# Softmax batches without the exponential function: power of two times a squared quartic, spread over three engines

## The chip, the cores and the metric

One core of one Trainium2 chip runs the whole program. The metric is device time in microseconds (us) of one execution; lower is better. Engines are named as in the profile: PE (TensorE matmul), PEld (its weight load), DVE (VectorE), ACT (ScalarE), POOL (GpSimd), SP (the queue that issues the DMAs).

## The reference

```
x: 8 x 4096 x 192      weight_gen: 8 x 4096 x 8 heads x 7 taps
w   = softmax(weight_gen, axis=-1)               # exp(w - max) / (sum + 1e-9)
out[b, s, h] = sum_k w[b, s, h, k] * x_pad[b, s + k, h]     # a 7-tap filter over the sequence
h   = out.reshape(32768, 192) @ w_in             # w_in 192 x 2048
y   = (h * cos(h)) @ w_out                       # w_out 2048 x 192
```

## The kernel before, in words

Each of the 128 partitions holds 256 consecutive rows of the sequence. The work goes in 64 blocks of 4 rows a partition. A block passes these stages:

- **Softmax** (`softmax`, L187): taps of 16 rows, so of four blocks, are loaded at once (a tile of 128x896). DVE finds the maximum of each 7 taps (L200), POOL subtracts it (L202), ACT takes the exponential in place (L205), POOL sums the taps (`add_taps`, L181 and L184) and scales the sum (L213), DVE takes the reciprocal (L216), POOL multiplies (L222). Three small early batches fill the start; fifteen "steady" ones follow, with `early=False`.
- **Filter** (`attention`, L244): on POOL, for a block, seven products (L257) and six sums (L272), 13 instructions in all; the last sum completes the tile `xa`.
- **Transpose**: PE transposes `xa` row by row (L316) into spare columns of the accumulator `acc` of the output matmul; ACT copies `acc` to `part` (L439), ACT and POOL split the transposed rows into `x_hi` (L297) and `x_lo` (L299).
- **First matmul** for a pair of 128-column chunks of w_in (L337 and L354, into `h`), eight pairs a block, 512 pairs in all; then h*cos(h): ACT rounds (L364), DVE takes the fraction (L368), ACT the cosine by its sine function (L372), DVE multiplies (L375), ACT and DVE split the product into `ghi` (L382) and `glo` (L386).
- **Second matmul** (`ffn_out`, L416), six pairs later (`LAG = 6`), then `evacuate`: the copy to `part`, and on POOL the sums `part` (L456) and `fin` (L457).

The order of each engine's instructions is the order in which the Python code issues them; a manual dependency at the end fixes it. The main loop goes over pairs `i`. In each pass it issues ACT's and DVE's work on earlier pairs, then `products()` (PE), then one `next(sm)` when the pair's `step` is in `SOFTMAX`, then two steps of the filter, `next(bg)`. `step` counts the pairs from 0 to 31 within a cycle of four blocks; each steady softmax batch begins at step 0 and feeds the four blocks whose transposes start at step 22 of that cycle and 8, 16 and 24 pairs later. The filter of a block may be issued only when its taps are `ready` (set after L222) and when the block two before is transposed. `until_mixed` (L487) issues whatever is missing of a block's filter just before its first transpose.

ACT holds one function table at a time: the exponential and the sine are in different ones. At step 6 (`EXP`) the kernel issues a table load, the exponential and a load back (the two rows `ACT_TABLE_LOAD` at L205 and L372). Around it the order is changed by hand: at step 7 `products()` is issued earlier, at steps 8 to 10 PE's second matmul is cut in two, and at steps 7 to 9 the splits are held back.

Of the kernel before, what the change touches and what calls it, by code (L numbers as in the profile page):

```python
# [11 lines left out]
F32 = mybir.dt.float32  # L12
F32R = mybir.dt.float32r
I32 = mybir.dt.int32
# [23 lines left out]


F64_SCALE = 2.0 ** -112  # L40


@with_exitstack
def tile_softmax_conv_then_cos_ffn(
# [133 lines left out]
    def add_taps(t, out):  # L178
# [4 lines left out]
        for more in (three[:, :, 1], three[:, :, 2], t[:, :, 6]):  # L183
            nc.gpsimd.tensor_tensor(out=out, in0=old, in1=more, op=ALU.add)  # L184
            old = out

    def softmax(r0, r1, eng, early=True, to=None):  # L187
        n = (r1 - r0) * H
        if r0 == 0:
            t = const.tile([P, n, K], F32, name="taps0")  # L190
        else:
            tile_ = work.tile([P, RW * H, K], F32, name="taps")
            t = tile_[:, 0:n, :]
        nc.sync.dma_start(out=t.rearrange("p a k -> p (a k)"), in_=g_v[:, :, r0 * H * K:r1 * H * K])
        for b in range(r0 // R, r1 // R):
            taps[b] = t.rearrange("p (r h) k -> p r h k", h=H)[:, b * R - r0:(b + 1) * R - r0]
        yield
        top_ = work.tile([P, RW * H], F32, name="top")
        top = top_[:, 0:n]
        nc.vector.tensor_reduce(out=top, in_=t, axis=AX.X, op=ALU.max)  # L200
        yield
        eng.tensor_tensor(  # L202
            out=t, in0=t, in1=top.unsqueeze(2).broadcast_to([P, n, K]), op=ALU.subtract)
        yield
        nc.scalar.activation(out=t, in_=t, func=AF.Exp)  # L205
        yield
        den_ = work.tile([P, RW * H], F32, name="den")
        den = den_[:, 0:n]
        if early:
            nc.vector.tensor_reduce(out=den, in_=t, axis=AX.X, op=ALU.add)  # L210
        else:
            add_taps(t, den)
        (nc.vector if early else nc.gpsimd).tensor_scalar(  # L213
            out=den, in0=den, scalar1=1e-9, scalar2=TWO_PI, op0=ALU.add, op1=ALU.mult)
        yield
        nc.vector.reciprocal(out=den, in_=den)  # L216
        yield
        m = 0 if to is None else to.shape[1]
        if m:
            eng.tensor_tensor(  # L220
                out=to, in0=t[:, 0:m], in1=den[:, 0:m].unsqueeze(2).broadcast_to([P, m, K]), op=ALU.mult)
        eng.tensor_tensor(  # L222
            out=t[:, m:], in0=t[:, m:], in1=den[:, m:].unsqueeze(2).broadcast_to([P, n - m, K]),
            op=ALU.mult)
        ready.update(range(r0 // R, r1 // R))
# [18 lines left out]
    def attention(b, eng, ra=0, rb=R, home="pr", t=None, acc=None):  # L244
        xt = rows[b]
        if t is None:
            t = taps[b][:, ra:rb]
        n = rb - ra
        if b not in mixed:
            xa_ = work.tile([P, R, D], F32, name="xa")  # L250
            mixed[b] = xa_
        xa = mixed[b][:, ra:rb]
        if acc is None:
            acc = xa

        def product(k, dst):
            eng.tensor_tensor(  # L257
                out=dst.rearrange("p r (h g) -> p r h g", h=H),
                in0=xt[:, k + ra:k + rb, :].rearrange("p r (h g) -> p r h g", h=H),
                in1=t[:, :, :, k:k + 1].broadcast_to([P, n, H, G]), op=ALU.mult)  # L260

        product(0, acc)
        yield
        old = None
        for k in range(1, K + 1):
            if k < K:
                pr = work.tile([P, R, D], F32, name="pr", tag=home,
                               bufs={"pr": 2, "turn": TMP, "part0": 3}[home])
                product(k, pr[:, ra:rb])
                yield  # L270
            if old is not None:
                eng.tensor_tensor(out=acc if k < K else xa, in0=acc, in1=old[:, ra:rb], op=ALU.add)  # L272
                yield
            old = pr
# [53 lines left out]
    def ffn_in_first(i, h=None):  # L328

        b, pair = divmod(i, NPAIR)  # L330
        x_hi, x_lo = xT[b]
        if h is None:
            h = ps_h.tile([P, 2, CT], F32, name="h")
        for m, (w, v) in enumerate(((wa_hi, x_lo), (wa_lo, x_hi), (wa_hi, x_hi))):
            for q in range(2):
                rs = slice(q * D2, (q + 1) * D2)
                nc.tensor.matmul(  # L337
                    h[:, q, :], lhsT=w[rs, chunk(pair, q)], rhs=v[rs, q, :],
                    start=(m == 0), stop=False, skip_group_check=True)
        hs[i] = h  # L340
        traded(h)
# [86 lines left out]
    def evacuate(j):  # L428
        b, m = divmod(j, 2 * R)
        half, m = divmod(m, R)  # L430
        tp, s = divmod(m, 2)
        if s == 0:
            return
        group = j // 2
        acc = accs.pop(group)
        bt = group // R + 2
        part = work.tile([P, 2, CT], F32, name=f"part{half}", bufs=(3 if half == 0 else 2))
        if WHOLE < bt < NB:
            nc.scalar.copy(out=part, in_=acc)  # L439
            r = group % R  # L440
            splits.append(split(bt, part[:, :, 2 * D:], slice(r * P, (r + 1) * P), nc.gpsimd))
        else:
            nc.scalar.copy(out=part[:, :, 0:2 * D], in_=acc[:, :, 0:2 * D])
        part = part[:, :, 0:2 * D]
        if half == 0:
            sums[(b, tp)] = part
            return
        if tp == 0:
            fin_t = work.tile([P, R, D], F32, name="fin")
            finals[b] = fin_t  # L450
        fin = finals[b]
        old = sums.pop((b, tp))
        last = b == NB - 1
        eng = nc.vector if last else nc.gpsimd
        ts = slice(2 * tp, 2 * tp + 2)
        eng.tensor_tensor(out=part, in0=part, in1=old, op=ALU.add)  # L456
        eng.tensor_tensor(out=fin[:, ts, :], in0=part[:, :, 0:D], in1=part[:, :, D:2 * D],  # L457
                          op=ALU.add)
        if tp == 1 or last:
            t0 = 2 * tp if last else 0  # L460
            def store(t0=t0):
                nc.sync.dma_start(out=o_v[:, :, (b * R + t0) * D:(b * R + 2 * tp + 2) * D],
                                  in_=fin[:, t0:2 * tp + 2, :].rearrange("p r d -> p (r d)"))

            if last:
                store()
            else:
                stores[j + LATE] = store
        if tp == 1:
            finals.pop(b)  # L470
            for pair in range(NPAIR):
                g_parts.pop(b * NPAIR + pair)
# [94 lines left out]
    N = NB * NPAIR  # L567

    sm = sm2
    EXP = 6  # L570
    SOFTMAX = (0, 2, 3, EXP, 7, 12, 13)
    for i in range(N + LAG + 1):
        b, pair = divmod(i, NPAIR)
        j = i - LAG
# [3 lines left out]
        if step == 0 and b + 4 < NB:  # L578
            r0 = (b + 4) * R
            sm = softmax(r0, min(r0 + RW, RPP), nc.gpsimd, early=False)  # L580
        busy = b + 4 < NB if step < NPAIR else b + 3 < NB
        exps = busy and step == EXP
        converts_now = converts.get(i, ())
        if converts_now:
            make_room()
# [8 lines left out]
        def products():  # L594
            if b < NB and pair == 0:
                assert b in transposed
            if whole is not None and j >= 0:

                ffn_out(j)
                ffn_in_first(i, whole)  # L600
            elif busy and EXP + 2 <= step <= EXP + 4:

                ffn_out(j, rest=False)
                ffn_in_first(i)
                ffn_out(j, rest=True)
            else:
                if i < N:
                    ffn_in_first(i, whole)
                if j >= 0:
                    ffn_out(j)  # L610
            if i < N:
                ffn_in_second(i)
            if j in stores:
                stores.pop(j)()
            if j >= 0:
                evacuate(j)


        early_sums = busy and step == EXP + 1
        if 0 <= i - 1 < N:  # L620
            act_turns(i - 1)
        if early_sums:
            products()
        if 0 <= i - 2 < N:
            act_hi(i - 2)
        all_of(*converts.pop(i - 1, ()))
        if exps:
            next(sm)
        now, later = [], []
        if not (busy and EXP + 1 <= step <= EXP + 3):  # L630
            now = list(splits)
            splits.clear()
        if whole is not None:
            t = work.tile([P, 2, CT], F32, name="part0", bufs=3)
            nc.scalar.copy(out=t, in_=whole)
            later.append(split(b + 1, t, slice(0, CT), nc.vector))
        if 0 <= i - 1 < N:
# [12 lines left out]
        all_of(*now)  # L650
        if i == N + LAG:
            break
        if not early_sums:
            products()
        load_weights(i)
        if step in SOFTMAX and step != EXP or NPAIR - 2 <= i < NPAIR + 1:
            next(sm, None)
        for _ in range(3 if i < 12 or i < 64 and i % 4 == 0 else 2):
            next(bg, None)
# [41 lines left out]
```

## Time and profile before

| | |
|---|---|
| median of 3 runs | 2301.77 us (2301.21 to 2303.03) |
| span of the profiled execution | 2300.3 us, 1.5 us under that median |
| PE busy | 2215.2 us, 96% of the span |
| POOL busy | 2002.3 us, 87% |
| DVE busy | 1905.0 us, 83% |
| ACT busy | 1897.5 us, 82% |
| ACT table loads at L205 and L372 | 15 and 15, 1283 ns each |

The page gives busy time by engine and granted clock by slice. The timeline lists an engine's instructions with their start in us from the span's start, their length, and in brackets the idle time ahead of one and what ended it. Idle time of an engine that others do not wait for costs nothing.

### The profile page before, as it was taken

How to read it: one execution, taken by the hardware profiler on the slowest of the kernel's cores; microseconds unless marked ns; L12 is line 12 of the kernel's file. 1: busy time of each engine (PE TensorE's matmuls, PEld its weight loads, DVE VectorE, ACT ScalarE, POOL GpSimd, SP SyncE). 2: the span in 40 equal slices, each digit the busy share in tenths (PEclk: the TensorE clock that was granted, in tenths of full speed). 3: DMA queues.
4: the chain of work that ended last, by engine and by line, in shares of the span. 5: the costliest groups of instructions: out<-in, count | busy, mean ns of one | idle time of the engine just before them, and what ended most of it. 6: DMA issues, size and time to landing. Idle time of an engine off the chain costs nothing.

```text
span 2300.3 us, 60609 instructions
## 1 busy us (share of the span) xinstructions
PE 2215.2 (96%) x26504; PEld 1993.6 (87%) x26504; DVE 1905.0 (83%) x1646; ACT 1897.5 (82%) x2131; POOL 2002.3 (87%) x1461
## 2 busy tenths in 40 slices
PE   3799999999999999999999999999999999999998
PEld 2588998889888888998989988898888889899897
DVE  7788888888888888888888888888888888888886
ACT  4588888888888888888888888888888888888885
POOL 8699989999999989989899899989989899899840
PEclk8799999999999999999999999999999999999999
DMA  6211221211211211211211212212211212212100
GB/s 154 56 43 40 50 51 33 58 41 34 58 39 44 50 40 44 50 49 34 58 33 43 58 31 52 50 32 52 50 41 42 58 26 50 57 26 52 33 9 22
DMA packets 25767, 105.55 MB, mean 46 GB/s; under 512 B 2734, under 2 KB 6566, under 8 KB 25502
## 3 DMA queue, kind: packets, MB, share of 16 engines
q1 hardware_dynamic: 25502, 101.67, 18.5%
q8 instruction: 208, 3.41, 0.6%
q14 instruction: 57, 0.47, 0.1%
HBM read 76.50 MB, written 25.17 MB: 44 GB/s over the span
## 4 chain that ended last, share of the span: by engine, by line
PE 56%; POOL 22%; ACT 11%; DVE 7%; issue 4%; DMA 0%; SPq 0%; POOLq 0%; ACTq 0%; DVEq 0%
PE acc L416 26%; PE h L354 19%; PE h L337 10%; POOL pr L257 6%; POOL xa L272 6%; DVE turn L368 3%; ACT part L439 3%; ACT turn L364 3%; POOL part L456 3%; DVE glo L386 2%; POOL x_lo L299 2%; POOL xa L257 2%; POOL fin L457 2%; ACT turn L372 2%; ACT ghi L382 1%
## 5 line engine op out<-in xcount | busy, mean ns | idle before, releaser
L368 DVE TENSOR_TENSOR turn<-h,turn 128x1024 f32<-128x1024 f32 x512 | 625.8, 1222 | 309.9 <-ACT turn L364 309.9
L416 PE MATMUL acc<-wo,ghi 64*128 64x384 f32 x8144 | 815.2, 336 | 16.6 <-ACT part L439 13.5
L416 PEld LDWEIGHTS acc<-wo,ghi 64*128 64x128 f32 x8144 | 739.2, 185 | 64.2 <-ACT part L439 26.7
L272 POOL TENSOR_TENSOR xa<-xa,pr 128x768 f32<-128x768 f32 (+1 forms) x384 | 704.0, 1833 | 0.7
L372 ACT ACTIVATE turn<-turn 128x1024 f32<-128x1024 f32 x512 | 543.7, 1062 | 181.0 <-DVE turn L368 177.7
L375 DVE SCALAR_TENSOR_TENSOR h<-h,turn 128x1024 f32<-128x1024 f32 x512 | 631.0, 1232 | 54.2 <-ACT turn L372 54.2
L364 ACT ACTIVATE turn<-h 128x1024 int32<-128x1024 f32 x512 | 525.6, 1027 | 165.0 <-PE h L354 164.2
L386 DVE TENSOR_TENSOR glo<-h,ghi 128x1024 bf16<-128x1024 f32 x512 | 622.4, 1216 | 9.9 <-ACT ghi L382 9.9
L257 POOL TENSOR_TENSOR pr<-xt,taps 128x768 f32<-128x768 f32 (+1 forms) x384 | 588.2, 1532 | 11.9
L382 ACT CAST ghi<-h 128x1024 fp32r<-128x1024 f32 x512 | 518.2, 1012 | 15.5 <-DVE h L375 15.5
L416 PE MATMUL acc<-wo_b,glo 64*128 64x192 bf16 x8144 | 435.6, 243 | 0.0
L456 POOL TENSOR_TENSOR part<-part,part 128x768 f32<-128x768 f32 x126 | 233.0, 1849 | 183.0 <-ACT part L439 156.7
L416 PEld LDWEIGHTS <-glo 64*128 64x128 bf16 x8144 | 333.8, 94 | 28.5 <-issue 13.7
L337 PE MATMUL h<-x_lo,wa_hi 64*128 64x512 f32 x1024 | 216.4, 410 | 37.0 <-DVE glo L386 28.4
L354 PE MATMUL h<-x_lo,wa_hi 64*128 64x512 f32 x1024 | 251.1, 478 | 0.6
L439 ACT COPY part<-acc 128x1024 f32<-128x1024 f32 x244 | 242.9, 996 | 0.0
L354 PE MATMUL h<-x_lo,wb_hi 64*128 64x512 f32 x1024 | 209.4, 397 | 0.0
L354 PE MATMUL h<-x_hi,wa_hi 64*128 64x512 f32 x1024 | 209.1, 396 | 0.0
L337 PE MATMUL h<-x_hi,wa_hi 64*128 64x512 f32 x1024 | 208.1, 394 | 0.0
L337 PE MATMUL h<-x_hi,wa_lo 64*128 64x512 f32 x1024 | 207.4, 392 | 0.0
L354 PE MATMUL h<-x_hi,wb_hi 64*128 64x512 f32 x1024 | 206.9, 391 | 0.0
L354 PE MATMUL h<-x_hi,wb_lo 64*128 64x512 f32 x1024 | 206.4, 391 | 0.0
(69 smaller groups left out, 2097.7 us busy)
## 6 DMA issues: line engine op xcount, KB each, us to landing
xt<-in_x_dram SPq DMA_DIRECT2D x62, 960.0 KB, 6.9
out_dram<-fin SPq DMA_DIRECT2D x63, 384.0 KB, 3.4
taps<-in_weight_gen_dram SPq DMA_DIRECT2D x15, 448.0 KB, 4.7
raw<-in_moe_w_out_dram SPq DMA_DIRECT2D x8, 384.0 KB, 4.2
raw<-in_moe_w_in_dram SPq DMA_DIRECT2D x10, 256.0 KB, 10.0
xt<-in_x_dram SPq DMA_DIRECT2D x1, 768.0 KB, 10.3
xt<-in_x_dram SPq DMA_DIRECT2D x1, 540.0 KB, 5.7
raw<-in_moe_w_in_dram SPq DMA_DIRECT2D x4, 128.0 KB, 5.6
```

Source lines behind the costliest of these rows:

```text
L257: eng.tensor_tensor(out=dst.rearrange("p r (h g) -> p r h g", h=H), in0=xt[:, k + ra:k + rb, :].rearrange("p r (h g) -> p r h g", h=H), in ...
L272: eng.tensor_tensor(out=acc if k < K else xa, in0=acc, in1=old[:, ra:rb], op=ALU.add)
L337: nc.tensor.matmul(h[:, q, :], lhsT=w[rs, chunk(pair, q)], rhs=v[rs, q, :], start=(m == 0), stop=False, skip_group_check=True)
L354: nc.tensor.matmul(h[:, 1 - q, :], lhsT=w[rs, cs], rhs=v[rs, q ^ middle, :], start=False, stop=(m == len(prods) - 1), skip_group_check=True)
L364: nc.scalar.activation(out=t.bitcast(I32), in_=hs[i], func=AF.Identity, bias=0.25, scale=1.0)
L368: nc.vector.tensor_tensor(out=t, in0=hs[i], in1=t.bitcast(I32), op=ALU.subtract)
L372: nc.scalar.activation(out=t, in_=t, func=AF.Sin, bias=SIN_BIAS, scale=SIN_SCALE)
L375: nc.vector.scalar_tensor_tensor(out=hs[i], in0=hs[i], scalar=TWO_PI, in1=turns.pop(i), op0=ALU.mult, op1=ALU.mult)
L382: nc.scalar.copy(out=hi, in_=hs[i])
L386: nc.vector.tensor_tensor(out=lo, in0=hs.pop(i), in1=hi.bitcast(F32), op=ALU.subtract)
L416: nc.tensor.matmul(to, lhsT=g[rs, n, t * P:(t + 1) * P], rhs=w[rs, fc, :], start=(lo == 0 and c == 0 and (whole or s == 0)), stop=(lo == 1 ...
L439: nc.scalar.copy(out=part, in_=acc)
```

## The change

For the fifteen steady batches the exponential of t (t is at most 0) is computed as follows: n = t / ln 2 rounded to an integer, r = t - n ln 2, a quartic in r/2 as the product of two squared terms with constants added, squared once more, times 2^n, whose bits ACT makes by a scale and a bias. A constant factor that stays in the taps cancels in the division. Early batches keep the exponential. The steps are spread over one pair each.

```
+    def powers(t):
+        nc.scalar.activation(out=whole, in_=t, func=AF.Identity, scale=1.0 / LN_2)
+        yield
+        nc.vector.scalar_tensor_tensor(
+            out=t, in0=whole, scalar=-LN_2, in1=t, op0=ALU.mult, op1=ALU.add)
+        yield
+        nc.scalar.activation(out=side, in_=t, func=AF.Square, bias=a1, scale=0.5)
+        yield
+        nc.scalar.activation(out=t, in_=t, func=AF.Square, bias=a2, scale=0.5)
+        yield
+        nc.vector.tensor_scalar(out=side, in0=side, scalar1=b1, scalar2=None, op0=ALU.add)
+        yield
+        nc.scalar.activation(out=whole, in_=whole, func=AF.Relu, bias=ONE_BITS, scale=2.0 ** 23)
+        yield
+        nc.vector.scalar_tensor_tensor(
+            out=t, in0=t, scalar=b2, in1=side, op0=ALU.add, op1=ALU.mult)
+        yield
+        nc.scalar.activation(out=t, in_=t, func=AF.Square)
+        yield
+        nc.gpsimd.tensor_tensor(out=t, in0=t, in1=whole.bitcast(F32), op=ALU.mult)
+        yield
...
-        yield
-        nc.scalar.activation(out=t, in_=t, func=AF.Exp)
-        yield
+        if early:
+            yield
+            nc.scalar.activation(out=t, in_=t, func=AF.Exp)
+            yield
+        else:
+            eng.tensor_scalar(
+                out=t, in0=t, scalar1=0.0, scalar2=EXP_LEAST, op0=ALU.min, op1=ALU.max)
+            yield
+            yield from powers(t)
...
-    EXP = 6
-    SOFTMAX = (0, 2, 3, EXP, 7, 12, 13)
+    SOFTMAX = (0, 1, 2, 4, 5, 6, 8, 9, 10, 11, 12, 13, 14, 16, 18)
```

The tiles `whole` and `side` are new with one buffer each; `top` goes from two buffers to one and `part0` from three to two. The special order around step 6 (`EXP`, `exps`, `early_sums`, the held-back splits, the cut second matmul) is removed, so every pair is issued alike.

With the new list the batch's last step, L222 before, is issued at step 18 where it was at step 13.

ACT around the exponential, before: rows of steps 6 and 7. In the names, `turn` and `ghi` are the work of the cosine.

```order
L364 ACTIVATE turn<-h 128x1024
L382 CAST ghi<-h 128x1024
L205 ACT_TABLE_LOAD
L205 ACTIVATE taps<-taps 128x896
L372 ACT_TABLE_LOAD
L372 ACTIVATE turn<-turn 128x1024
L297 CAST x_hi<-part_17943 128x2x128
```

ACT at the same place of the program with the change, from the end of step 4; `whole` is the first of the five new ACT instructions, `side` the second.

```order
L338 CAST x_hi<-part_17885 128x2x128
L200 ACTIVATE whole<-taps 128x896
L405 ACTIVATE turn<-h 128x1024
L423 CAST ghi<-h 128x1024
L413 ACTIVATE turn<-turn 128x1024
L480 COPY part_18024<-acc 128x1024
```

The pair of table loads with the exponential between is gone, and one ACT instruction stands behind the `x_hi` of each of the steps 4, 6, 8, 10 and 12.

POOL at steps 13 to 18, before: the `fin` of step 13, then the batch's last multiplication (L222), then the filter of the batch's first block.

```order
L457 TENSOR_TENSOR fin<-part_14016 128x384
L222 TENSOR_TENSOR taps<-taps,den 128x896
L257 TENSOR_TENSOR xa<-xt,taps 128x768
L257 TENSOR_TENSOR pr<-xt,taps 128x768
L299 TENSOR_TENSOR x_lo<-part_14016,x_hi 128x2x128
```

POOL from the same `fin` on with the change.

```order
L498 TENSOR_TENSOR fin<-part_14073 128x384
L218 TENSOR_TENSOR taps<-taps,whole 128x896
L340 TENSOR_TENSOR x_lo<-part_14073,x_hi 128x2x128
L188 TENSOR_TENSOR three<-taps 128x384
L191 TENSOR_TENSOR den<-three 128x128
L191 TENSOR_TENSOR den<-den,three 128x128
L191 TENSOR_TENSOR den<-den,taps 128x128
L253 TENSOR_SCALAR den<-den 128x128
L340 TENSOR_TENSOR x_lo<-part_14215,x_hi 128x2x128
L340 TENSOR_TENSOR x_lo<-part_14351,x_hi 128x2x128
L263 TENSOR_TENSOR taps<-taps,den 128x896
L298 TENSOR_TENSOR xa<-xt,taps 128x768
```

The last multiplication (now L263) and the first product behind it moved behind the `x_lo` rows of steps 14, 16 and 18, which stood behind them before.

POOL at the end of that block's filter, before; the `x_lo` row is that of step 20, the first `part` and `fin` are those of step 19, the second those of step 21.

```order
L272 TENSOR_TENSOR xa_14021<-xa_14021,pr_14303 128x768
L456 TENSOR_TENSOR part1_14439<-part1_14439,part0_14158 128x2x384
L457 TENSOR_TENSOR fin_14441<-part1_14439 128x384
L272 TENSOR_TENSOR xa_14021<-xa_14021,pr_14373 128x768
L299 TENSOR_TENSOR x_lo_14173<-part1_14439,x_hi_14172 128x2x128
L456 TENSOR_TENSOR part1_14575<-part1_14575,part0_14301 128x2x384
L457 TENSOR_TENSOR fin_14441<-part1_14575 128x384
L257 TENSOR_TENSOR xa_14579<-xt_14163,taps_13104 128x768
```

And with the change, from the second `part` on.

```order
L497 TENSOR_TENSOR part1_14631<-part1_14631,part0_14351 128x2x384
L498 TENSOR_TENSOR fin_14490<-part1_14631 128x384
L298 TENSOR_TENSOR pr_14635<-xt_13656,taps_13159 128x768
L313 TENSOR_TENSOR xa_14421<-xa_14421,pr_14563 128x768
L298 TENSOR_TENSOR pr_14638<-xt_13656,taps_13159 128x768
L313 TENSOR_TENSOR xa_14421<-xa_14421,pr_14635 128x768
L298 TENSOR_TENSOR pr_14641<-xt_13656,taps_13159 128x768
L313 TENSOR_TENSOR xa_14421<-xa_14421,pr_14638 128x768
L313 TENSOR_TENSOR xa_14421<-xa_14421,pr_14641 128x768
L340 TENSOR_TENSOR x_lo_14225<-part1_14631,x_hi_14224 128x2x128
L298 TENSOR_TENSOR xa_14712<-xt_14566,taps_13159 128x768
```

Before, the block's last sum stood ahead of the `part` of step 21; now it is the seventh row behind that step's `fin`, ahead of the next block's first product.

More of the change, by code (lines that the diff above doesn't have):

```diff
@@ L40 @@
 F64_SCALE = 2.0 ** -112
+EXP_A = ((0.2721300161859934, 6.259058152201904), (1.7341319627121385, 0.787141348722592))
+EXP_UNIT = 0.04161451162765518 ** 2
+EXP_LEAST = -100.0
+LN_2 = math.log(2.0)
+ONE_BITS = float(127 * 2 ** 23)
 @with_exitstack
@@ L185, in add_taps @@
             old = out
+    def powers(t):
+        (a1, b1), (a2, b2) = EXP_A
+        whole_ = work.tile([P, RW * H, K], I32, name="whole", bufs=1)
+        side_ = work.tile([P, RW * H, K], F32, name="side", bufs=1)
+        whole, side = whole_[:, 0:t.shape[1]], side_[:, 0:t.shape[1]]
+        nc.scalar.activation(out=whole, in_=t, func=AF.Identity, scale=1.0 / LN_2)
[18 more added lines that the diff above has]
+        yield
     def softmax(r0, r1, eng, early=True, to=None):
@@ L197, in softmax @@
         yield
-        top_ = work.tile([P, RW * H], F32, name="top")
+        top_ = work.tile([P, RW * H], F32, name="top", bufs=1)
         top = top_[:, 0:n]
@@ L213, in softmax @@
         (nc.vector if early else nc.gpsimd).tensor_scalar(
-            out=den, in0=den, scalar1=1e-9, scalar2=TWO_PI, op0=ALU.add, op1=ALU.mult)
+            out=den, in0=den, scalar1=1e-9 / (1.0 if early else EXP_UNIT), scalar2=TWO_PI,
+            op0=ALU.add, op1=ALU.mult)
         yield
@@ L267, in attention @@
                 pr = work.tile([P, R, D], F32, name="pr", tag=home,
-                               bufs={"pr": 2, "turn": TMP, "part0": 3}[home])
+                               bufs={"pr": 2, "turn": TMP, "part0": 2}[home])
                 product(k, pr[:, ra:rb])
@@ L436, in evacuate @@
         bt = group // R + 2
-        part = work.tile([P, 2, CT], F32, name=f"part{half}", bufs=(3 if half == 0 else 2))
+        part = work.tile([P, 2, CT], F32, name=f"part{half}", bufs=2)
         if WHOLE < bt < NB:
@@ L580, in tile_softmax_conv_then_cos_ffn @@
             sm = softmax(r0, min(r0 + RW, RPP), nc.gpsimd, early=False)
-        busy = b + 4 < NB if step < NPAIR else b + 3 < NB
-        exps = busy and step == EXP
         converts_now = converts.get(i, ())
@@ L600, in products @@
                 ffn_in_first(i, whole)
[L601 to L605, printed above, removed]
             else:
@@ L616, in products @@
                 evacuate(j)
-        early_sums = busy and step == EXP + 1
         if 0 <= i - 1 < N:
             act_turns(i - 1)
-        if early_sums:
-            products()
         if 0 <= i - 2 < N:
@@ L626, in tile_softmax_conv_then_cos_ffn @@
         all_of(*converts.pop(i - 1, ()))
[L627 to L632, printed above, removed]
+        later = []
+        now = list(splits)
+        splits.clear()
         if whole is not None:
-            t = work.tile([P, 2, CT], F32, name="part0", bufs=3)
+            t = work.tile([P, 2, CT], F32, name="part0", bufs=2)
             nc.scalar.copy(out=t, in_=whole)
@@ L652, in tile_softmax_conv_then_cos_ffn @@
             break
-        if not early_sums:
-            products()
+        products()
         load_weights(i)
-        if step in SOFTMAX and step != EXP or NPAIR - 2 <= i < NPAIR + 1:
+        if step in SOFTMAX or NPAIR - 2 <= i < NPAIR + 1:
             next(sm, None)
```

## Prediction

> **What bounds the kernel now.** I read the page first.
>
> ```profile
> span 2300.3 us, 60609 instructions
> PE 2215.2 (96%) x26504; PEld 1993.6 (87%) x26504; DVE 1905.0 (83%) x1646; ACT 1897.5 (82%) x2131; POOL 2002.3 (87%) x1461
> PEclk8799999999999999999999999999999999999999
> ```
>
> PE is busy 96% of the span at full granted clock, so a gain can only come out of PE's small remainder; POOL, at 87%, is the next to be late. Next, PE's timeline in a quiet stretch (seven pairs lie between these two pair starts), then around one exponential, step 7 to step 11 of the cycle, with two copies of ACT waited for and, later, an `x_lo` of POOL.
>
> ```profile
> 1238.04 0.43 PE L337 MATMUL h<-x_lo,wa_hi 64*128 64x512 f32 x2
> 1267.77 0.42 PE L337 MATMUL h<-x_lo,wa_hi 64*128 64x512 f32 x2
> ...
> 1167.62 0.40 PE L337 MATMUL h<-x_lo,wa_hi 64*128 64x512 f32 x2
> 1168.31 1.57 PE L416 MATMUL acc<-wo,ghi 64*128 64x384 f32 x16
> 1172.32 1.67 PE L416 MATMUL acc<-wo,ghi 64*128 64x384 f32 x16 [0.29 <-ACT part L439]
> 1182.23 1.67 PE L416 MATMUL acc<-wo,ghi 64*128 64x384 f32 x16 [0.63 <-ACT part L439]
> 1186.60 0.42 PE L337 MATMUL h<-x_lo,wa_hi 64*128 64x512 f32 x2
> 1208.26 0.49 PE L337 MATMUL h<-x_lo,wa_hi 64*128 64x512 f32 x2 [0.25 <-POOL x_lo L299]
> ```
>
> A quiet pair takes (1267.77 - 1238.04) / 7 = 4.247 us. Around the exponential four pairs take 1186.60 - 1167.62 = 18.98 us, 2.0 over 4 x 4.247. The whole cycle is seen in the rows of the table loads, one for each of the fifteen steady batches:
>
> ```profile
> L205 ACT ACT_TABLE_LOAD  x15: 1283/1283/1283, 196.7 to 2134.4; - x15
> ```
>
> (2134.4 - 196.7) / 14 = 138.4 us a cycle against 32 x 4.247 = 135.9: the exponential and all that goes with it cost PE **2.5 us a batch, 15 x 2.5 = 37 us** in all. That is the most that removing it can bring. Last, POOL's and PE's timelines from the batch's last multiplication (L222) to the first transpose of the block that it feeds, at step 22.
>
> ```profile
> 1202.62 1.77 POOL L222 TENSOR_TENSOR taps<-taps,den 128x896 f32<-128x896 f32 x1
> 1204.46 1.54 POOL L257 TENSOR_TENSOR xa<-xt,taps 128x768 f32<-128x768 f32 x1
> ...
> 1226.35 1.83 POOL L456 TENSOR_TENSOR part<-part,part 128x768 f32<-128x768 f32 x1
> 1228.26 1.03 POOL L457 TENSOR_TENSOR fin<-part 128x384 f32<-128x384 f32 x1
> 1229.25 1.85 POOL L272 TENSOR_TENSOR xa<-xa,pr 128x768 f32<-128x768 f32 x1
> 1231.06 0.74 POOL L299 TENSOR_TENSOR x_lo<-part,x_hi 128x256 fp32r<-128x256 f32 x1
> ...
> 1233.81 0.41 PE L337 MATMUL h<-x_lo,wa_hi 64*128 64x512 f32 x2
> 1235.92 0.23 PE L316 MATMUL acc<-ident,xa 64*128 64x64 f32 x2
> ...
> 1237.04 1.55 POOL L257 TENSOR_TENSOR xa<-xt,taps 128x768 f32<-128x768 f32 x1
> ```
>
> POOL needs 1229.25 + 1.85 - 1202.62 = 28.5 us from the start of L222 to the block's last sum, and ends it at 1231.10. PE, whose step 22 begins at 1233.81, reads the sum at 1235.92. So this chain has **4.8 us of slack**, about one pair. This is the view that decides my forecast.
>
> **The change part by part.**
>
> *The table loads and the exponential go.* ACT's rows at steps 6 and 7:
>
> ```profile
> 1164.49 1.01 ACT L382 CAST ghi<-h 128x1024 fp32r<-128x1024 f32 x1
> 1165.52 1.28 ACT L205 ACT_TABLE_LOAD   x1
> 1166.82 0.96 ACT L205 ACTIVATE taps<-taps 128x896 f32<-128x896 f32 x1
> 1167.79 1.28 ACT L372 ACT_TABLE_LOAD   x1
> 1169.09 1.06 ACT L372 ACTIVATE turn<-turn 128x1024 f32<-128x1024 f32 x1
> ```
>
> They hold up the cosine by 1169.09 - 1165.52 = 3.6 us; 2.5 of it and of the late `x_lo` reaches PE. Nothing else fills that place, so the 2.5 us come back. The Trainium skill, "ScalarE: Activation LUTs", section "What ACT_TABLE_LOAD costs", adds a drain of about 1.38 us to each load, 2.66 us a switch. Here each row begins 0.02 us behind the load ahead of it, so no drain shows; by the page the delay would be 6.3 us a batch, and by these rows it is 3.6.
>
> *Five ACT instructions and three on DVE come in,* at steps 4 to 12. The nearest ACT row is the exponential, 0.96 us for the same tile, some 0.1 of it overlapped as with its neighbours. For DVE the nearest is the maximum over a tile of that size, and above it the operations on `h`:
>
> ```profile
> L200 DVE TENSOR_REDUCE top<-taps 128x128 f32<-128x896 f32 x15 | 16.1, 1076 | 0.0
> L368 DVE TENSOR_TENSOR turn<-h,turn 128x1024 f32<-128x1024 f32 x512 | 625.8, 1222 | 309.9 <-ACT turn L364 309.9
> ...
> 1220.33 0.39 ACT L297 CAST x_hi<-part 128x256 fp32r<-128x256 f32 x1
> 1221.29 1.03 ACT L364 ACTIVATE turn<-h 128x1024 int32<-128x1024 f32 x1 [0.57 <-PE h L354]
> 1224.58 1.00 ACT L439 COPY part<-acc 128x1024 f32<-128x1024 f32 x1
> ```
>
> ACT has 0.57 us of idle time behind the `x_hi` of an even step and none in an odd one, so each new 0.87 us leaves it 0.3 us later: 1.5 us after five. DVE idles 310 / 512 = 0.6 us a pair, so 1.1 us put into a pair holds the cosine up by about 0.5 us there. PE forgives little: the copy ends at 1225.58, and the next second matmul starts 1168.31 - 1167.62 = 0.69 us into its pair; that pair starts at 1233.81 - 2 x 4.247 = 1225.32, so 0.43 us of lateness are free. Delay of 1.5 us, half a us more where DVE's instructions fall, less 0.4: I put 1.2 us a batch on PE, between 0 (all absorbed) and 2.5 (no better than the exponential). With the 2.5 us that come back, **the gain of this half is 1.3 us a batch**, from 0 to 2.5.
>
> *On POOL the batch's end moves by five steps.* The clamp, new at step 2, costs POOL between nothing and the 1.77 us of L222 on the same tile; it delays the sum of the block before, and a chain with 4.8 us of slack takes that. From step 13 on the product with `whole`, the sums over the taps and the scaling stand in a stretch where POOL now has no filter to work on, since no block has `ready` taps; the wait for what follows covers them. The last multiplication stands behind the `x_lo` of step 18, and that waits for ACT's `x_hi` of that step: step 18 begins at 1233.81 - 4 x 4.247 = 1216.82, and its `x_hi` is the row above, ended at 1220.72. With 0.74 us for the `x_lo` POOL starts the multiplication at 1221.5 instead of 1202.62, **18.9 us later**, on the clock of these rows. The way from there to the last sum has the same 14 instructions, but the order shows one `x_lo` in it instead of four (3 x 0.7 us less) and two `part` and `fin` instead of one (2.9 us more, from the start of that `part` to the next row): 28.5 + 0.8 = 29.3 us. The last sum so ends at 1221.5 + 29.3 = 1250.8. PE reads it at 1235.92 and can do nothing else, since its queue is in order: behind the transpose stand the rest of that pair and all later ones, and ACT and DVE then starve. **PE waits 14.8 us a batch.** The bounds are 13.3 and 16.3: 5% of the 29.3 us, since POOL runs beside other work there than in these rows.
>
> *PE's clock after such a wait.* At the program's start PE resumes after a wait of 3.64 us; the same work, first matmul to the second half of the first, stands there again a pair later:
>
> ```profile
> 95.00:101.50 6.50, 5.17 (x38) 4.73 (x40) 4.00 (x6) 1.89 (x4) 6.24 (x5) 0.50 0.00 0
> 101.50:108.00 6.50, 6.50 (x75) 5.72 (x72) 3.32 (x3) 4.70 (x7) 3.32 (x3) 0.99 0.43 96
> ...
> 96.33 0.80 PE L337 MATMUL h<-x_lo,wa_hi 64*128 64x512 f32 x2 [3.64 <-DVE glo L386]
> 101.52 0.53 PE L354 MATMUL h<-x_lo,wa_hi 64*128 64x512 f32 x2
> 103.03 0.41 PE L337 MATMUL h<-x_lo,wa_hi 64*128 64x512 f32 x2
> 105.76 0.49 PE L354 MATMUL h<-x_lo,wa_hi 64*128 64x512 f32 x2
> ```
>
> The granted clock is 0.50 in the first stretch and 0.99 in the second; the work takes 101.52 - 96.33 = 5.2 us against 2.7. A wait four times as long should do the same: **2.4 us a batch**, from 0 (it does not drop) to 3.2 (all 6.5 us of the first stretch at half speed). The Trainium skill, "TensorE: Matmul & The Clock Gate", section "What's actually happening", lifts the half clock after about 3.4 us of busy time, which would cost 1.7 us a batch and 10 us less in all; the row here has 5.2 us of it.
>
> *The rest has one answer.* `part0` loses a buffer: its two tiles are read by POOL before the wait is over, so ACT's copies find them free. The special order of steps 7 to 10 goes with the exponential and is in the 2.5 us. The next block's filter starts an `x_lo`, 0.7 us, behind the end of the wait; now it starts 1237.04 - 1235.92 = 1.1 us behind that transpose. On SP the load of the block's rows moves behind a store, whose `fin` POOL has done by then, and it lands in 6.9 us, issued while POOL is in the middle of the 29 us chain. Two more rows carry this and the next sum:
>
> ```profile
> L222 POOL TENSOR_TENSOR taps<-taps,den 128x224 f32<-128x224 f32 x1 | 0.6, 577 | 0.0
> ...
> xt<-in_x_dram SPq DMA_DIRECT2D x62, 960.0 KB, 6.9
> ```
>
> The sum: 15 x (14.8 + 2.4 - 1.3) = 238.5 us, less 1.2 us because the last batch's L222 is on a quarter of the tile (0.58 us, not 1.77), so 237 us on the span of 2300.3. The median is 1.5 us above the span: **2539 us**.
>
> **The rivals.**
>
> *POOL's chain does not bind (faster, 5%).* If PE's first transpose did not need this filter at step 22, only the other half would be left: 15 x 1.3 = 19.5 us less, 2282 us (2265 with all 2.5). It decides at L222's start: later than 4.8 us is too late, and the order says 18.9. Against it: the chain above, where every link is a row. The page's 2.66 us a switch, all on PE's path, would be 80 us for thirty switches and a time near 2220; the 37 us that the cycle shows over quiet pairs exclude it.
>
> *The wait without the clock (7%).* The same 14.8 us, but the granted clock stays at 1.0: 15 x 2.4 = 36 us less, 2503 us. For it: only the start, where PE works in short pieces, shows the drop.
>
> *The lateness is handed on (6%).* The filter of the next block is issued later too, with one more product, sum and `x_lo` (1.5 + 1.9 + 0.7 = 4.1 us) behind the `part` of step 27, which waits for ACT. If its slack is now 4.8 us, 0.7 are left. Should it miss by 3 us, 15 x 3 = 45 us come on top: 2584 us.
>
> *The new instructions eat the gain and no more (2%).* With ACT and DVE costing PE 2.5 us and no wait on POOL: 2302 us.
>
> **How the numbers follow.** My forecast has the remaining 80%. With all low ends it would be 15 x (13.3 + 0 - 2.5) = 162 us more, with all high ends 15 x (16.3 + 3.2) = 292; that they all meet is unlikely, so I take 2495 to 2585, which takes in the second and third rival. A measurement of this kernel tells about 0.2%, 5 us, from no change. Faster: the first rival and no other, 0.05. Same: 0.01. Slower: 0.94.
>
> **What would show it.** PE's idle time ahead of the transposes (L316 before) named to POOL's `xa` sum, about fifteen times 15 us; a granted clock that drops fifteen times; only the first two table loads left; and cycles near 154 us instead of 138.4. If the transposes wait for nothing, or POOL starts the last multiplication before step 15, the forecast is wrong.

## The result and the profile after

The changed kernel takes **2580.9 us** (median of four runs, 2579.1 to 2583.6) against 2302.4 us (four runs of the kernel before, 2301.2 to 2304.6): 1.1214 times the time before, 95% interval 1.1198 to 1.123. That is slower by 278.5 us, 18.6 us for each of the fifteen steady batches. The forecast was 2539 us, with a range of 2495 to 2585.

The page of the changed kernel: its span, the busy times and the granted clock.

```profile
span 2578.8 us, 60741 instructions
PE 2249.4 (87%) x26504; PEld 2007.5 (78%) x26504; DVE 1992.7 (77%) x1691; ACT 1896.8 (74%) x2161; POOL 2067.9 (80%) x1491
PEclk8899898998989989899998989989899898999989
```

Every engine's share has fallen, PE's from 96% to 87%: they wait for each other. The clock has dips all along the program where it had them at the start only. In the list of waits the first row is the one that the forecast named; the second was there before with 28.4 us, 22 times.

```profile
PE acc L357 <- POOL xa L313: 228.8, 15, 15.4
PE h L378 <- DVE glo L427: 61.2, 38, 6.5
```

PE waits 228.8 / 15 = **15.25 us** a batch for POOL's last `xa` sum. The start and the end of that chain, on POOL and then on PE:

```profile
1197.23 0.74 POOL L340 TENSOR_TENSOR x_lo<-part,x_hi 128x256 fp32r<-128x256 f32 x1 [7.75 <-ACT x_hi L338]
1197.92 1.77 POOL L263 TENSOR_TENSOR taps<-taps,den 128x896 f32<-128x896 f32 x1
...
1224.09 3.68 POOL L313 TENSOR_TENSOR xa<-xa,pr 128x768 f32<-128x768 f32 x2
```

```profile
1227.82 0.37 PE L357 MATMUL acc<-ident,xa 64*128 64x64 f32 x2 [15.32 <-POOL xa L313]
1229.17 0.77 PE L395 MATMUL h<-x_lo,wa_hi 64*128 64x512 f32 x2
1231.54 0.40 PE L378 MATMUL h<-x_lo,wa_hi 64*128 64x512 f32 x2
1233.65 0.22 PE L357 MATMUL acc<-ident,xa 64*128 64x64 f32 x2
```

POOL sat idle for 7.75 us, waited for ACT's `x_hi`, and only then began the batch's last multiplication: the order, not the amount of work, made it late. From there to the last sum went 1224.09 + 3.68 - 1197.92 = 29.85 us (29.3 forecast). The first pair after the wait then takes 1233.65 - 1227.82 = 5.83 us instead of 4.247, 1.6 us more, with the clock down. The same stretch in the table of windows (columns: stretch, length, busy time of PE, PEld, DVE, ACT and POOL with instruction counts, granted clock, DMA share, GB/s):

```profile
1214.50:1228.00 13.50, 0.18 (x4) 0.18 (x6) 0.57 (x1) 0.00 (x0) 13.19 (x10) 0.61 0.00 0
1228.00:1231.30 3.30, 3.30 (x28) 2.79 (x28) 0.00 (x0) 0.00 (x0) 3.30 (x3) 0.53 0.00 0
1231.30:1236.00 4.70, 4.70 (x58) 4.25 (x56) 3.20 (x3) 3.88 (x5) 3.45 (x3) 1.00 0.00 0
```

So far all as forecast. What was not: the place of the new instructions. PE's pair starts of steps 6, 7, 12, 13 and 15 of one cycle:

```profile
1138.19 0.40 PE L378 MATMUL h<-x_lo,wa_hi 64*128 64x512 f32 x2
1143.78 0.50 PE L378 MATMUL h<-x_lo,wa_hi 64*128 64x512 f32 x2 [1.18 <-DVE glo L427]
...
1165.70 0.50 PE L378 MATMUL h<-x_lo,wa_hi 64*128 64x512 f32 x2
1171.61 0.50 PE L378 MATMUL h<-x_lo,wa_hi 64*128 64x512 f32 x2 [1.32 <-DVE glo L427]
...
1180.54 0.40 PE L378 MATMUL h<-x_lo,wa_hi 64*128 64x512 f32 x2
```

The nine pairs take 42.35 us instead of 9 x 4.247 = 38.22: **4.1 us a batch lost, where I had put 1.2.** Most of it sits in two pairs, steps 6 and 12 (5.59 and 5.91 us), and in both of them PE waits for DVE. In the rows grouped by line (the two numbers behind the count are busy us and mean ns of one), the two new instructions of DVE that run there, and the third that came in, at step 10:

```profile
L202 DVE SCALAR_TENSOR_TENSOR taps<-whole,taps 128x896 f32<-128x896 int32 x14 | 36.4, 2601 | 0.0
L213 DVE SCALAR_TENSOR_TENSOR taps<-taps,side 128x896 f32<-128x896 f32 x14 | 36.4, 2601 | 0.0
L209 DVE TENSOR_SCALAR side<-side 128x896 f32<-128x896 f32 x14 | 14.4, 1031 | 0.0
```

The first two take 2.60 us, and I had put 1.1, which only the third keeps. What runs on POOL at that moment shows why; step 6, POOL, DVE, and ACT's cosine, which waits for DVE:

```profile
1138.67 1.85 POOL L497 TENSOR_TENSOR part<-part,part 128x768 f32<-128x768 f32 x1 [0.90 <-ACT part L480]
1138.86 2.60 DVE L202 SCALAR_TENSOR_TENSOR taps<-whole,taps 128x896 f32<-128x896 int32 x1
1140.59 1.75 POOL L498 TENSOR_TENSOR fin<-part 128x384 f32<-128x384 f32 x1
...
1142.63 1.06 ACT L413 ACTIVATE turn<-turn 128x1024 f32<-128x1024 f32 x1 [2.21 <-DVE turn L409]
```

DVE's instruction begins 0.2 us behind POOL's `part` and ends 0.94 us after it; POOL's `fin`, 1.03 us before the change, takes 1.75 us. It reads as if DVE had to wait until POOL's running instruction was over, and POOL's next one until DVE's was. The cosine idled 2.21 us for it, where the quiet pairs show about 0.4.

The theory after this reading: of the 18.6 us a batch, 15.25 are the wait for the last sum, 1.6 the half clock behind it, and 4.1 - 2.5 = 1.6 the new instructions over the exponential that went; together 18.5. And of the 4.1 us nearly all is DVE and POOL in each other's way, not the amount of new work. The rivals, each tried below: that the wait is not due to the order but to POOL's load (so that an earlier start does not help); that ACT's five instructions cost the 4.1 us; that the two-input instruction is simply slow; that the loss behind the wait is the refilling of the stages, not the clock.

### The profile page after: what moved, and what is told of

Read it like the earlier page. It is cut to its first block, busy times and chain, and to the rows that moved or that the text cites. A ratio compares the mean times of both kernels' runs of the same rounds, so it can differ in the third digit from the quotient of the medians.

```text
span 2578.8 us, 60741 instructions
## 1 busy us (share of the span) xinstructions
PE 2249.4 (87%) x26504; PEld 2007.5 (78%) x26504; DVE 1992.7 (77%) x1691; ACT 1896.8 (74%) x2161; POOL 2067.9 (80%) x1491
## 4 chain that ended last, share of the span: by engine, by line
PE 39%; POOL 21%; DVE 18%; ACT 11%; issue 10%; DMA 1%; SPq 0%; ACTq 0%; POOLq 0%; DVEq 0%
PE acc L457 18%; PE h L395 14%; DVE turn L409 9%; PE h L378 6%; POOL xa L313 6%; ACT turn L405 5%; POOL pr L298 5%; POOL part L497 3%; DVE glo L427 3%; DVE h L416 2%; ACT part L480 2%; POOL fin L498 2%; POOL x_lo L340 2%; DVE taps L202 1%; DVE taps L213 1%
## 5 line engine op out<-in xcount | busy, mean ns | idle before, releaser
L409 DVE TENSOR_TENSOR turn<-h,turn 128x1024 f32<-128x1024 f32 x512 | 625.5, 1222 | 556.6 <-ACT turn L405 556.5
L340 POOL TENSOR_TENSOR x_lo<-part,x_hi 128x256 fp32r<-128x256 f32 x244 | 180.6, 740 | 285.5 <-ACT x_hi L338 285.5
L457 PEld LDWEIGHTS <-glo 64*128 64x128 bf16 x8144 | 343.6, 96 | 17.8 <-issue 3.7
L357 PE MATMUL acc<-ident,xa 64*128 64x64 f32 x976 | 111.8, 218 | 228.8 <-POOL xa L313 228.8
L378 PE MATMUL h<-x_lo,wa_hi 64*128 64x512 f32 x1024 | 219.0, 415 | 66.4 <-DVE glo L427 61.2
L395 PE MATMUL h<-x_lo,wa_hi 64*128 64x512 f32 x1024 | 254.6, 486 | 0.6
L357 PEld LDWEIGHTS acc<-ident,xa 64*128 64x128 f32 x976 | 73.1, 139 | 233.6 <-POOL xa L313 233.6
L395 PE MATMUL h<-x_hi,wa_hi 64*128 64x512 f32 x1024 | 209.8, 398 | 0.0
```

The lines of the kernel that those rows point to most:

```text
L378: nc.tensor.matmul(h[:, q, :], lhsT=w[rs, chunk(pair, q)], rhs=v[rs, q, :], start=(m == 0), stop=False, skip_group_check=True)
L395: nc.tensor.matmul(h[:, 1 - q, :], lhsT=w[rs, cs], rhs=v[rs, q ^ middle, :], start=False, stop=(m == len(prods) - 1), skip_group_check=True)
L409: nc.vector.tensor_tensor(out=t, in0=hs[i], in1=t.bitcast(I32), op=ALU.subtract)
L457: nc.tensor.matmul(to, lhsT=g[rs, n, t * P:(t + 1) * P], rhs=w[rs, fc, :], start=(lo == 0 and c == 0 and (whole or s == 0)), stop=(lo == 1 ...
```

## The experiments

Each edit is made to the changed kernel, if nothing else is said, and each ratio is to the kernel before, timed on the same chip.

**e1_early8: every steady batch begins eight pairs earlier.** Nothing else moves.

```diff
+    EARLIER = 8
-        step = i % (SB * NPAIR) - (SB - 1) * NPAIR
+        step = (i + EARLIER) % (SB * NPAIR) - (SB - 1) * NPAIR
...
```

> The changed kernel with every steady batch begun one block, eight pairs, earlier; the same instructions and the same distances between them. Theory (the wait at step 22 comes from the place where the last multiplication is issued): the transposes wait under 1 us in all, the clock stays at 1.0 behind the start, a cycle falls from 157.1 to 140.0 us, so 15 x 17.1 = 257 us less: 2324 us. What is left over the kernel before, some 22 us, is the work of ACT and DVE. Rival (POOL is simply too slow for the new work, wherever it is issued): the wait moves and most of the 278 us stay, over 2500 us.

Measured: 2355.4 us, ratio 1.0228 (1.0212 to 1.0243). The wait for `xa` has gone from the list, and the mean granted clock is 0.989 as before the change, where the changed kernel has 0.949:

```profile
core 0: 2353.2 us, clock 0.989
...
PE h L378 <- POOL x_lo L340: 20.4, 28, 1.0
```

The wait comes from where the batch's end stands in POOL's order: that is shown, since 225 of the 278 us go when the place alone is changed. But the time is 31 us over the 2324 that I expected. The wait for `x_lo` above is new: at two steps of fourteen batches, 7 and 15 of the cycle, POOL comes late to an `x_lo`, since it works through the batch's instructions and the filter without a pause. PE's weight loads, which come just ahead, show the wait fuller:

```profile
PEld h L378 <- POOL x_lo L340: 32.7, 28, 1.4
```

In one cycle the two pairs take 5.15 and 5.08 us instead of 4.247, and the pair behind each 0.1 us more than that: 1.9 us a batch, 14 x 1.9 = 27 of the 31 us that I had missed.

**e2_nostt: both two-input instructions of DVE left out.** The remainder r and the product of the two quadratics are not computed; the order is that of the changed kernel.

```diff
-        nc.vector.scalar_tensor_tensor(
-            out=t, in0=whole, scalar=-LN_2, in1=t, op0=ALU.mult, op1=ALU.add)
...
-        nc.vector.scalar_tensor_tensor(
-            out=t, in0=t, scalar=b2, in1=side, op0=ALU.add, op1=ALU.mult)
```

> The changed kernel without its two scalar_tensor_tensor instructions on DVE; so the remainder r and the product of the two quadratics are left out. Theory (each of them stands 2.6 us on DVE because it waits for a POOL instruction, and that is most of what steps 6 to 14 lose): the loss there falls from 4.1 us a batch to about 1.2, 15 x 2.9 = 43 us less: 2538 us. Rival (the five ACT instructions make the loss): it falls by under 1 us a batch, 2566 us or more.

Measured: 2532.2 us, ratio 1.0994 (1.0976 to 1.1012). (2580.9 - 2532.2) / 15 = 3.2 us a batch come back, 6 us more in all than I expected. In PE's list of waits the one for `xa` is as it was; below it stand the pair starts of steps 6 and 15 of one cycle:

```profile
PE acc L353 <- POOL xa L309: 228.9, 15, 15.4
PE h L374 <- DVE glo L423: 25.8, 8, 6.7
...
1115.62 0.42 PE L374 MATMUL h<-x_lo,wa_hi 64*128 64x512 f32 x2
1154.11 0.40 PE L374 MATMUL h<-x_lo,wa_hi 64*128 64x512 f32 x2
```

The waits for DVE fall from 61.2 to 25.8 us and from 38 to 8. The nine pairs take 1154.11 - 1115.62 = 38.49 us instead of 42.35, so 3.9 of the 4.1 us are gone there. The five ACT instructions, all still there, are cleared: for them and for DVE's third instruction 0.3 us is left. That the time shows 3.2 us and not 3.9 is in part due to the wait: the pair of step 22 and the one behind it are 0.4 us longer here than in the changed kernel.

**e3_probe: a third two-input instruction where POOL is idle.** It stands at step 17, in POOL's gap of 8 us ahead of the `x_lo` of step 18. It reads `whole`, as L202 does, and `side`, as L213 does.

```diff
+            nc.vector.scalar_tensor_tensor(
+                out=side, in0=whole, scalar=0.0, in1=side, op0=ALU.mult, op1=ALU.add)
...
```

> The changed kernel with one more scalar_tensor_tensor of the same shape and types on DVE, issued at step 17, where POOL is idle between two x_lo. Theory (it waits for POOL's running instruction, then runs): the added one takes 1.0 to 1.1 us, the two others 2.6 us as before. Rival (this form with all operands in SBUF is slow by itself): 2.6 us for all three. The time moves by under 10 us.

The rows grouped by line, same operation and same shape three times (L264 is the probe), and one probe with POOL's row behind the gap:

```profile
L204 DVE SCALAR_TENSOR_TENSOR taps<-whole,taps 128x896 f32<-128x896 int32 x14 | 36.5, 2604 | 0.0
L215 DVE SCALAR_TENSOR_TENSOR taps<-taps,side 128x896 f32<-128x896 f32 x14 | 36.4, 2602 | 0.0
L264 DVE SCALAR_TENSOR_TENSOR side<-whole,side 128x896 f32<-128x896 int32 x14 | 15.2, 1082 | 0.0
...
1195.53 1.08 DVE L264 SCALAR_TENSOR_TENSOR side<-whole,side 128x896 f32<-128x896 int32 x1
1199.22 0.74 POOL L348 TENSOR_TENSOR x_lo<-part,x_hi 128x256 fp32r<-128x256 f32 x1 [8.03 <-ACT x_hi L346]
```

1.08 us with POOL idle, 2.60 with POOL at work: the instruction is not slow, it waits. The two others wait 3.0 us a batch on DVE, out of the 3.9 us that PE loses by them (e2). (A single run took 2590.4 us, 9.5 more than the changed kernel.)

**e4_warm: PE kept at work during the wait.** At step 22 the first sixteen matmuls of the second matmul are done ten times; the repeats write the same values.

```diff
+    AGAIN = 9
...
+        fed = j > 2 * R and j % (2 * R) == 0 and (j // (2 * R)) % SB == 1 and group // R + 2 < NB
+        turns_ = [0] * (AGAIN if fed else 0) + [0, 1]
+        for at, lo in enumerate(turns_):
-        for lo in range(2):
...
```

> The changed kernel, where PE at step 22 does the first sixteen matmuls of that second matmul ten times in all ahead of the transposes (each time from a fresh start, so the sum is the same): nine more of 1.57 us each, 14.1 us, fill the wait of 15.3. Theory (of the 17.1 us that step 22 is longer, 15.3 are the wait and 1.9 the half clock behind it): the granted clock stays at 1.0 and the time falls by 15 x 1.9 = 28 us to 2552 us. Rival (the 1.9 us are the pipeline filling again): no change, 2581 us.

Measured: 2583.9 us, ratio 1.1219 (1.1202 to 1.1236): nothing gained. The reason is in the wait that was left and the window behind it:

```profile
PE acc L357 <- POOL xa L313: 41.9, 15, 2.9
```

```profile
1226.00:1231.30 5.30, 2.46 (x38) 2.14 (x38) 0.00 (x0) 0.00 (x0) 5.22 (x5) 1.00 0.02 3
1231.30:1235.00 3.70, 3.70 (x22) 2.93 (x20) 0.28 (x1) 1.34 (x2) 3.70 (x3) 0.54 0.00 0
```

PE was still idle for 2.8 us, and that was enough: the clock fell at 1231.3, 0.9 us after PE had started again (at 1230.4), for about 3.4 us. The trial did not take away what it was to take away, so it says nothing about the two theories, and it was done again.

**e5_warm11: the same with two repeats more,** `AGAIN = 11`.

> As the changed kernel, but at step 22 PE does the first 16 matmuls of the second matmul twelve times instead of once (the repeats write the same values), so that it works through all of its 15.3 us wait for POOL's sum: eleven repeats of 1.39 us are 15.3 us. Theory (the loss behind the wait, 1.9 us a batch, is the half clock): the granted clock stays at 1.0, step 22 loses 15.3 us and not 17.1, and the time falls by 15 x 1.8 = 27 us to about 2554 us. Rival (the loss is the refilling of the stages behind PE, which starve during the wait whatever the clock is): about 2581 us with the clock at 1.0.

Measured: 2561.8 us, ratio 1.1135 (1.1119 to 1.115). The windows of one wait, with PE busy and the clock at 1.00 throughout, and PE's first two transposes behind it:

```profile
1204.00:1220.00 16.00, 16.00 (x184) 15.74 (x180) 3.17 (x3) 1.81 (x3) 15.69 (x10) 1.00 0.00 1
1220.00:1226.00 6.00, 5.93 (x80) 5.29 (x80) 2.41 (x3) 3.08 (x4) 6.00 (x6) 1.00 0.01 3
```

```profile
1220.13 0.27 PE L357 MATMUL acc<-ident,xa 64*128 64x64 f32 x2
1224.45 0.22 PE L357 MATMUL acc<-ident,xa 64*128 64x64 f32 x2
```

The first pair now takes 4.32 us instead of 5.83: the 1.5 us were the clock, and with it they go. The whole program gains 19.1 us, 1.3 a batch, between the two expectations and nearer to the clock's. The refilling of the stages behind PE, which starved as before, costs next to nothing.

**e6_early8_nostt: e1 and e2 together** (the remainder and the product are left out here too).

> Every steady batch begins eight pairs earlier, and both scalar_tensor_tensor instructions on DVE are left out (so the remainder r and the product of the two quadratics are not computed). Theory (the terms add: wait for the last sum gone, wait of DVE for POOL's port gone, left are the late x_lo of some 1.7 us a batch and 0.3 us for ACT): 2264 us without any loss, plus 15 x 2.0 = 30, so about 2294 us, faster than the kernel before. Rival (the two are not independent, POOL is late for its own work in the early place and the losses move elsewhere): 2315 us or more.

Measured: 2296.3 us, ratio 0.9982 (0.9973 to 0.9991), 2 us from the expectation: the terms add. (The gains of e1 and e2 as timed, 225 and 49 us, would have given 2307. About 6 of these 10 us are the 0.4 us a batch by which e2's wait had grown; the rest is of the size of the intervals.) The row that is left is that of e1, unchanged:

```profile
PE h L374 <- POOL x_lo L336: 20.4, 28, 1.0
```

**e7_placed: the whole computation, placed by these findings.** The batch begins ten pairs earlier; each two-input instruction is issued in a pair in which POOL is about to idle; the sum over the taps goes from four POOL instructions to one reduction on DVE; POOL's remaining ones stand where the next `x_lo` has slack. In `powers`, L202 joins the step of L200, and the relu of L211 goes ahead of L209.

```diff
-        add_taps(t, den)
+        nc.vector.tensor_reduce(out=den, in_=t, axis=AX.X, op=ALU.add)
...
-    SOFTMAX = (0, 1, 2, 4, 5, 6, 8, 9, 10, 11, 12, 13, 14, 16, 18)
+    EARLIER = 10
+    SOFTMAX = (0, 2, 3, 6, 8, 10, 12, 13, 14, 16, 18, 19, 20, 21)
...
```

> The whole computation, placed by what the runs have shown: the batch begins ten pairs earlier, each two-input instruction on DVE is issued in a pair in which POOL is about to idle, the sum over the taps goes from POOL (five instructions) to one reduction on DVE, and no batch work of POOL stands ahead of an x_lo without slack. Theory: no wait for the last sum, no half clock, the two DVE instructions at about 1.1 us instead of 2.6, left over some 1 us a batch: 2264 + 15 = about 2280 us, 1% faster than the kernel before. Rival (POOL's port stays taken, since the instructions meet its part and fin wherever they stand; or the reduction on DVE holds the cosine up): 2303 us or more.

Measured: 2296.7 us, ratio 0.9978 (0.9969 to 0.9987). That is 0.2% faster than the kernel before, only a fifth of what was expected. PE's list of waits names POOL no more; the loss sits with an instruction that I had not suspected, the addition with one input. Rows grouped by line, then POOL and DVE around it:

```profile
L210 DVE TENSOR_SCALAR side<-side 128x896 f32<-128x896 f32 x14 | 28.4, 2028 | 0.0
L201 DVE SCALAR_TENSOR_TENSOR taps<-whole,taps 128x896 f32<-128x896 int32 x14 | 21.9, 1564 | 0.0
L212 DVE SCALAR_TENSOR_TENSOR taps<-taps,side 128x896 f32<-128x896 f32 x14 | 15.1, 1081 | 0.0
```

```profile
1153.19 1.85 POOL L493 TENSOR_TENSOR part<-part,part 128x768 f32<-128x768 f32 x1 [0.92 <-ACT part L476]
1155.11 1.29 POOL L494 TENSOR_TENSOR fin<-part 128x384 f32<-128x384 f32 x1
```

```profile
1153.38 2.14 DVE L210 TENSOR_SCALAR side<-side 128x896 f32<-128x896 f32 x1
```

It begins 0.2 us behind `part` and ends 0.48 us after it. So it, too, waits for POOL's running instruction, and takes about half a microsecond by itself; the 1.03 us of the changed kernel were half waiting. (In e2 its mean is 0.62 us.) Of the two placed instructions the second, L212, has its 1.08 us, on the tiles on which it took 2.60 before; the first, L201, still takes 1.56 in the mean: its place was not free of POOL. (In the cycle of these rows it ends 0.96 us after POOL's `fin`.)

**e8_add_act: that addition moved to ACT,** which has no instruction of the batch in that pair; the relu stands behind the last square.

```diff
-        nc.vector.tensor_scalar(out=side, in0=side, scalar1=b1, scalar2=None, op0=ALU.add)
+        nc.scalar.activation(out=side, in_=side, func=AF.Identity, bias=b1, scale=1.0)
...
```

> As e7_placed, but the one-input addition to side goes from DVE, where it took 2.03 us at its new place beside POOL's part (1.03 us in the changed kernel), to ACT as an Identity with a bias, in a pair in which ACT has no other instruction of the batch; the second two-input instruction stays where POOL idles (1.08 us). Theory (DVE waits for POOL's running instruction in this one-input operation too, and that is what steps 4 to 6 lose): their loss falls from 1.48 us to about 0.5 us, ACT's sixth instruction costs 0.06 us (0.3 us for five): 2296.7 - 15 x 0.9 = about 2283 us. Rival (steps 4 to 6 lose by the second two-input instruction or by ACT's chain): 2295 us or more.

Measured: **2285.1 us**, ratio 0.9937 (0.9923 to 0.995), 2 us from the expectation, and the fastest kernel of this study: 16 us (0.6%) less than the kernel before, 296 less than the change as it was made.

**e9_pair: the addition stays on DVE,** straight ahead of the second two-input instruction.

> As e7_placed, but the one-input addition stays on DVE and moves one pair later, straight ahead of the second two-input instruction, where POOL idles. Theory (the addition alone takes about 0.5 us, the rest of its 2.03 us was waiting for POOL's part): its row shows 0.5 us, the two together put 1.6 us into one pair of DVE instead of 3.1 us into two, and the loss of 1.48 us at steps 4 to 6 falls to about 0.8 us: 2296.7 - 15 x 0.7 = about 2286 us. Rival (the addition takes 1 us or more whatever POOL does): 2297 us or more.

Measured: 2294.4 us, ratio 0.9976 (0.9966 to 0.9986): no better than e7, 8 us over the expectation. By its time alone the run would fit the rival, whose 2297 us lie within the interval; the rows decide. POOL and DVE at that place:

```profile
1155.47 1.85 POOL L308 TENSOR_TENSOR xa<-xa,pr 128x768 f32<-128x768 f32 x1
1157.29 1.12 POOL L335 TENSOR_TENSOR x_lo<-part,x_hi 128x256 fp32r<-128x256 f32 x1
```

```profile
1156.93 0.88 DVE L210 TENSOR_SCALAR side<-side 128x896 f32<-128x896 f32 x1
1157.84 1.51 DVE L211 SCALAR_TENSOR_TENSOR taps<-taps,side 128x896 f32<-128x896 f32 x1
```

The pair came about a microsecond too early for POOL's gap, which begins behind the `x_lo`. The addition waited for the sum that ended at 1157.32 and ended 0.49 us after it, which held up the `x_lo` by 0.4 us (1.12 instead of 0.74 us); the second instruction then waited for the `x_lo`, to 1158.41, and ended 0.94 us later. Both rows agree with the mechanism to a tenth of a microsecond; it was the place that I had wrong, and the rival's size (the addition takes 1 us whatever POOL does) is excluded by 0.49.

## Why the prediction held, and which term was off

*The chain on POOL decides: right.* The start of the last multiplication after the `x_lo` of step 18, the length of the chain (29.85 us against 29.3) and PE's wait (15.25 us against 14.8) were read from the order and from rows of before, and e1 shows that the place alone makes the wait. The slack that the view of before gave, 4.8 us, was the right number to hold the 18.9 us against.

*The clock behind the wait: right in kind, 2.4 put, 1.6 found,* by the first pair's 5.83 us and e5's 1.5. I took a whole wait-and-resume of the program's start, where the low clock lasted longer than it does here: full clock is back 1231.3 - 1227.8 = 3.5 us after PE starts. The Trainium skill, "TensorE: Matmul & The Clock Gate", section "What's actually happening", lifts the half clock after about 3.4 us of busy time, and its 1.7 us a batch was the better figure; the trace agrees with it.

*The exponential's 2.5 us come back: right (e2's nine pairs are 0.3 us over quiet ones), but the sign of that half was wrong.* The term that failed is "1.1 us put into a pair": 1.2 us a batch for the new instructions, bounded by 2.5. It measured 4.1, so this half lost 1.6 us a batch instead of gaining 1.3. That alone is 15 x 2.9 = 43 us; the smaller clock term takes back 15 x 0.8 = 12, the longer wait adds 15 x 0.45 = 7. Together 38 of the 42 us between 2539 and 2581. That the time still lies in the range, 4 us under its upper end, is luck for this half: it went beyond its own bounds, a gain of 0 to 2.5 us, and the range held because it had room for a wait of 16.3 and a half clock of 3.2 us, which measured 15.25 and 1.6.

It was not the size alone. The 1.2 us were put together from 1.5 us of lateness on ACT and half a us on DVE, less 0.4. In e2 all five ACT instructions run and the nine pairs lose 0.3 us; the other 3.9 us hang on two instructions of DVE.

Why it failed: the rows by which I priced it do not have what the new instructions have. L200 before is a reduction of one tile, and L368 reads `h`, which is not in the memory of `taps` but where PE left it; both keep their speed beside POOL (1076 and 1222 ns before, the longest 1079 and 1227; 1075 and 1221 in e7). The new ones read two tiles of POOL's memory. e3 separates the two causes: 1.08 us alone, as I had put, and 1.5 of waiting. The Trainium skill, "SBUF — State Buffer", section "Who interferes with whom", has this: an instruction of VectorE with two inputs in SBUF, or a `tensor_scalar` in a mode that uses both ports, shares a port pair with GpSimd, and whichever is issued first holds it for its whole length, while `tensor_reduce` never contends. The rows here agree, for both kinds of instruction and in both directions (`fin` 1.75 instead of 1.03 us); in which mode the addition ran no run shows. It was the rule that spoke against the change, and I had not weighed it. The bound of 2.5 us should have been two waits for a POOL instruction of up to 1.85 us on top.

*The rivals.* That the chain does not bind is excluded by the 228.8 us. That the clock stays up is excluded by the windows. That the lateness is handed on: the list has no second row of `xa`, so the next block's slack of 0.7 us held; the time of 2581 lies near that rival's 2584 by chance. The rest (`part0` with one buffer less, the load behind a store, the next block's filter) added no wait.

What stays open: e8 still needs 137.5 us a cycle, by its rows of the first new instruction ((2074.8 - 150.3) / 14), against 135.9 for quiet pairs:

```profile
L200 ACTq EVENT_SEMAPHORE  x15: 17/17/17, 150.3 to 2074.8; - x15
```

These 1.6 us are spread over a dozen pairs and were not taken apart; DVE's two-input instructions still take 1.57 and 1.33 us there instead of 1.08. The 0.2 us a batch between e5's first pair (1.5 us won) and its time (1.3) lie in POOL's chain: with PE at work beside it, it takes 30.10 us from the start of L263 to the last sum in the wait shown, instead of 29.85.

## What to carry to other kernels

When an instruction is replaced by a longer chain of steps, look first at where the chain's last step lands in the order of the engine that hands the result on, and hold that lateness against the slack there: here the place cost 225 us, and the new instructions 4.1 x 15 = 62. Price a new DVE instruction by a row with the same number of inputs in the same memory, and beside the same neighbour: with POOL 80 to 90% busy, an instruction that has to share with it costs its own length plus the rest of what POOL is doing. Such work belongs on ACT where a form with one input will do, as in e8, or in a gap of POOL that is longer than the uncertainty of its start.

## What the runs showed of the hardware that I had not expected

A DVE instruction with two tiles of 128x896 in took 1.08 us with POOL idle and 2.60 us behind POOL's `part` (1.85 us); the one-input addition in float32 took 0.62 us (e2) to 2.14 us (e7) by the same cause, and POOL's own next instruction was held while DVE's ran (`fin` 1.75 us instead of 1.03). The granted clock fell to half after an idle time of PE of only 2.8 us (e4), not after PE's waits of 1.2 and 1.3 us for DVE at steps 6 and 12 of the changed kernel, where the windows around them show 1.00; where between the two it begins was not tried. In e4 it fell 0.9 us after PE had work again, so that the work behind the wait paid for all of it. Such dips are too short for the digits of the row `PEclk`: e4 has the same digits there as the kernel before, but a mean granted clock of 0.980 against 0.989.
